# Decode attention over a long cache: K loads of 64 KB a partition into an overlapping ring, in place of two of 32 KB

## The chip, the cores and the metric

One core of a Trainium2 chip. The metric is the device time of one execution in microseconds. The kernel before takes 1271.2 us (median). A profile's span is about 2 us shorter than the run's time.

## The reference

One query token attends to a cache of 65,536 tokens, 8 key/value heads of 256 elements, two query heads to each. K and V are 268 MB each, in bfloat16. Beside it stands a small MLP over the same 448 numbers, mixed in through a gate.

```python
q = (x @ wq)                                   # 16 heads of 256
scores = einsum("bhqd,bhkd->bhqk", q, k) * Dh ** -0.5
o = einsum("bhqk,bhkd->bhqd", softmax(scores), v)
a = o @ wo
b = gelu(layernorm(x) * w1 + b1) @ w2 + b2     # the small MLP ("mixer")
out = g * a + (1 - g) * b                      # g = sigmoid(sum(x * gate_w))
```

So 537 MB must be read once, and this kernel transposes each K tile on TensorE before the scores.

## The kernel before

The cache is walked in 32 tiles `j` of 16,384 tokens: 8 MB of K and 8 MB of V, 64 KB of each a partition. K comes in two loads of 32 KB a partition, one for each half of the ring. V is one load. All go through one queue, in this order (`DC` = 4 key blocks make half a tile, `BODY` = 8):

```python
kring = sb([P, 2, DC * NT, DH], bf16, "kring")        # 2 x 32 KB a partition
vbuf = sb([P, NV, DH], bf16, "vbuf")                  # 64 KB a partition
...
for j in range(NP):                                   # the queue's engine
    for a in range(2):
        if j >= 1:
            eng.wait_ge(sem_tr[NB - 1], BODY * (j - 1) + DC * (a + 1))
        eng.dma_start(kring[:, a]..., k_src(2 * j + a)).then_inc(sem_k[a], 16)
    if j == 0:
        eng.wait_ge(s_q, 1)
    else:
        eng.wait_ge(sem_pv, j)                        # values of j-1 are done
    ...
    eng.dma_start(vbuf[:, 0:n1, :]..., v_src(j, 0, n1)).then_inc(sem_v, 16)
    ...
```

TensorE does, for each tile, the keys (8 blocks, each of 16 transposes, whose copies to SBUF feed 32 score matmuls), then the values (128 matmuls). The last V is cut up: 96 of its 128 rows a partition come in one load, the rest in three small ones, whose values are computed last ("late values").

```python
def values(j, c0, u16):
    for r in range(BODY):                             # the softmax's denominators
        ...
        pe.matmul(acc[:, DENC:SELC], ones_sq[:, :], pT[:, r, :], ...)
    ...
    with pe.If(j < NP - 1):
        some(NLATE, NV)
    some(0, NLATE).then_inc(sem_pv, 1)                # 96 or 128 value matmuls in all
```

The softmax here doesn't subtract the row's maximum and nothing guards it: scores larger than these inputs give would overflow.

## Time and profile before

| | before |
|---|---|
| median | 1271.21 us (1270.63 to 1271.29) |
| span of the profile | 1269.2 us |
| main DMA queue | 99.6% of 16 engines' span |
| packets of K, 32 KB each | mean 1217.8 ns, 8192 of them |
| packets of V, 64 KB each | mean 2422.2 ns, 3968 of them |
| last packet of the last V load ends at | 1263.97 us |

The three lowest rows are counted from the packet records of the trace (start, duration and size of each). The same count shows at least 16 packets in flight, as many as there are DMA engines, all through the loop.

From the page of the kernel before: DMA's busy tenths in 40 slices, and the main queue (packets, MB, share of 16 engines' span).

```profile
DMA  9999999999999999999999999999999999999997
q1 hardware_dynamic: 16856, 544.22, 99.6%
```

Only the last slice is under nine tenths. The list of waits of the kernel before (who waited for what: us in total, times, longest us) shows the other side of it:

```profile
PE acc L310 <- DMA vbuf<-in_A_v_cache_dram: 172.5, 32, 6.3
PE kst L272 <- DMA kring<-in_A_k_cache_dram: 120.3, 30, 5.9
```

TensorE waits twice in nearly every one of the 32 tiles, for V (about 5.4 us, 32 times) and for K (about 4 us, 30 times). It has time to spare; bytes have not.

The end of the kernel before, from TensorE's timeline (start us, us, engine, line, operation, out<-in, count, and in brackets the idle time before and what ended it):

```profile
1225.45 4.90 PE L310 MATMUL acc<-vbuf,pT 128*2 128x256 bf16 x128 [6.11 <-DMA vbuf<-in_A_v_cache_dram]
1235.28 5.17 PE L272 MATMUL kst<-ident,kring 128*128 128x128 f32 x32 [4.93 <-DMA kring<-in_A_k_cache_dram]
...
1257.40 0.62 PE L302 MATMUL acc<-pT,ones_sq 128*128 128x32 bf16 x8
1259.46 4.08 PE L310 MATMUL acc<-vbuf,pT 128*2 128x256 bf16 x96 [1.44 <-DMA vbuf<-in_A_v_cache_dram]
1263.70 0.95 PE L328 MATMUL sps<-pT,vbuf 128*128 128x2 bf16 x32
```

Read from the top: values of the last but one tile; 4.93 us of rest until the last K's first half has landed; the last keys; 1.44 us of rest until the big part of the last V has landed; its 96 value matmuls; the late values. What comes after the last of the data is on the path, so this end counts microsecond for microsecond. The 96 matmuls ran at a mean granted clock of 0.67 (the PEclk column of this table of stretches; the columns are busy us of each engine with counts, then clock, DMA share and GB/s):

```profile
1259.40:1263.60 4.20, 4.08 (x96) 2.62 (x96) 0.00 (x0) 0.00 (x0) 0.00 (x0) 0.67 0.82 330
```

### The profile page before, as it was taken

How to read it: one execution, taken by the hardware profiler on the slowest of the kernel's cores; microseconds unless marked ns; L12 is line 12 of the kernel's file. 1: busy time of each engine (PE TensorE's matmuls, PEld its weight loads, DVE VectorE, ACT ScalarE, POOL GpSimd, SP SyncE). 2: the span in 40 equal slices, each digit the busy share in tenths (PEclk: the TensorE clock that was granted, in tenths of full speed). 3: DMA queues.
4: the chain of work that ended last, by engine and by line, in shares of the span. 5: the costliest groups of instructions: out<-in, count | busy, mean ns of one | idle time of the engine just before them, and what ended most of it. 6: DMA issues, size and time to landing. Idle time of an engine off the chain costs nothing.

```text
span 1269.2 us, 37707 instructions
## 1 busy us (share of the span) xinstructions
PE 940.7 (74%) x17033; PEld 862.6 (68%) x17033; DVE 408.2 (32%) x672; ACT 535.5 (42%) x779; POOL 0.9 (0%) x7
## 2 busy tenths in 40 slices
PE   3788776878767787668776687866778666886768
PEld 3677665777657776567776677756678566876657
DVE  2454343443213332223322233322233222342223
ACT  1455433554334553335533355433455233553335
POOL 0000000000000000000000000000000000000000
PEclk9888787887878897888978789878888788897889
DMA  9999999999999999999999999999999999999997
GB/s 411 420 432 439 434 430 421 437 434 439 432 420 437 433 439 434 420 434 435 440 434 428 422 437 434 438 430 424 437 432 439 432 424 431 436 438 432 432 423 337
DMA packets 16879, 544.39 MB, mean 429 GB/s; under 512 B 1887, under 2 KB 3937, under 8 KB 4324
## 3 DMA queue, kind: packets, MB, share of 16 engines
q1 hardware_dynamic: 16856, 544.22, 99.6%
q8 instruction: 8, 0.13, 0.0%
q14 instruction: 3, 0.02, 0.0%
q10 hardware_dynamic: 12, 0.01, 0.0%
HBM read 544.22 MB, written 0.00 MB: 429 GB/s over the span
## 4 chain that ended last, share of the span: by engine, by line
DMA 85%; PE 15%; issue 0%; ACTq 0%; DVE 0%; DVEq 0%
DMA vbuf<-in_A_v_cache_dram 84%; PE acc L310 14%; DMA b_b<-in_B_b_dram 1%; PE sps L377 0%; PE sps L328 0%; PE sps L379 0%; DVE stat L457 0%; ACTq L581 0%; PE sps L335 0%; PE prj L348 0%; ACTq L585 0%; DVE out_g L576 0%; DVEq L456 0%; ACTq L584 0%; ACTq L583 0%
## 5 line engine op out<-in xcount | busy, mean ns | idle before, releaser
L605 ACT ACTIVATE ktT<-kst 128x1024 bf16<-128x1024 bf16 x512 | 499.4, 1021 | 677.6 <-PE kst L272 677.2
L272 PE MATMUL kst<-ident,kring 128*128 128x128 f32 x4096 | 554.6, 296 | 129.9 <-DMA kring<-in_A_k_cache_dram 120.3
L272 PEld LDWEIGHTS kst<-ident,kring 128*128 128x128 f32 x4096 | 505.3, 154 | 139.0 <-issue 138.5
L515 DVE COPY ktT<-kst 128x1024 bf16<-128x1024 bf16 x512 | 354.1, 692 | 737.1 <-PE kst L272 715.2
L310 PE MATMUL acc<-vbuf,pT 128*2 128x256 bf16 x4064 | 179.5, 359 | 172.5 <-DMA vbuf<-in_A_v_cache_dram 172.5
L310 PEld LDWEIGHTS acc<-vbuf,pT 128*2 128x2 bf16 x4064 | 116.4, 109 | 229.2 <-DMA vbuf<-in_A_v_cache_dram 175.6
L284 PEld LDWEIGHTS sps<-qcur,ktT 128*128 128x128 bf16 x8192 | 238.1, 96 | 3.3 <-issue 0.7
L284 PE MATMUL sps<-qcur,ktT 128*128 128x2 bf16 x8192 | 236.8, 163 | 0.6 <-issue 0.6
L596 ACT ACTIVATE pT<-sps 128x32 bf16<-128x32 f32 x256 | 51.8, 202 | 12.4 <-PE sps L284 12.4
L520 DVE COPY accs<-acc 128x288 f32<-128x288 f32 x8 | 3.7, 458 | 91.1 <-PE acc L310 91.1
L302 PE MATMUL acc<-pT,ones_sq 128*128 128x32 bf16 x256 | 16.5, 178 | 3.2
L611 ACT ACTIVATE z_b<-z_b 128x896 bf16<-128x896 bf16 x7 | 6.6, 949 | 20.9 <-DVE z_b L503 20.9
L302 PEld LDWEIGHTS acc<-pT,ones_sq 128*128 128x128 bf16 x256 | 10.9, 96 | 6.4 <-ACT pT L596 6.4
L365 PE MATMUL acc<-ones_sq,gu 1*128 1x1 bf16 x42 | 1.3, 161 | 8.6 <-DMA b_b<-in_B_b_dram 8.6
L365 PEld LDWEIGHTS acc<-ones_sq,gu 1*128 1x128 bf16 x42 | 1.2, 99 | 8.7 <-DMA b_b<-in_B_b_dram 8.7
L340 PE MATMUL acc<-zrow,ones_sq 1*128 1x292 bf16 x9 | 2.7, 305 | 4.7 <-DVE accs L520 4.0
L340 PEld LDWEIGHTS acc<-zrow,ones_sq 1*128 1x128 bf16 x9 | 0.9, 97 | 7.4 <-DVE accs L520 6.1
L348 PE MATMUL prj<-wo_sb,oTn 128*1 128x112 bf16 x128 | 2.9, 211 | 3.2 <-DVE oTn L531 3.2
L508 DVE TENSOR_TENSOR gu<-wtmp,z_b 128x896 bf16 x7 | 4.4, 625 | 1.2 <-issue 1.2
L497 DVE TENSOR_TENSOR z_b<-wtmp,u_b 128x896 bf16<-128x896 bf16 x7 | 4.4, 626 | 0.5
L501 DVE TENSOR_TENSOR z_b<-u_b,wtmp 128x896 bf16<-128x896 bf16 x7 | 4.4, 625 | 0.5
L495 DVE TENSOR_TENSOR wtmp<-u_b 128x896 bf16<-128x896 bf16 x7 | 4.4, 625 | 0.5
(82 smaller groups left out, 73.5 us busy)
## 6 DMA issues: line engine op xcount, KB each, us to landing
kring<-in_A_k_cache_dram SPq DMA_DIRECT2D x64, 4096.0 KB, 27.5
vbuf<-in_A_v_cache_dram SPq DMA_DIRECT2D x1, 6144.0 KB, 29.0
wo_sb<-in_A_wo_dram SPq DMA_DIRECT2D x8, 448.0 KB, 32.2
vbuf<-in_A_wq_dram SPq DMA_DIRECT2D x1, 3072.0 KB, 10.4
vbuf<-in_A_v_cache_dram SPq DMA_DIRECT2D x1, 1024.0 KB, 31.1
vbuf<-in_A_v_cache_dram SPq DMA_DIRECT2D x1, 768.0 KB, 32.5
vbuf<-in_A_wq_dram SPq DMA_DIRECT2D x1, 512.0 KB, 11.2
vbuf<-in_A_v_cache_dram SPq DMA_DIRECT2D x31, 33.4
```

Of the source, the lines that this page charges most:

```text
L272: ins = pe.transpose(kst[:, b, j * P:(j + 1) * P], kring_f[:, a, r * NT + 4 * b + j, :], ident[:, :])
L284: ins = pe.matmul(sps[:, par, 2 * nt:2 * nt + 2], ktT[:, par, b, ntl * DH + dj:(ntl + 1) * DH:2], qcur[:, dj, :], start=(dj == 0), stop=(d ...
L302: pe.matmul(acc[:, DENC:SELC], ones_sq[:, :], pT[:, r, :], start=False, stop=(r == BODY - 1), skip_group_check=True)
L310: ins = pe.matmul(acc[o:o + REP, 0:DH], pT[:, r, 2 * nt:2 * nt + 2], vbuf[:, n, :], start=False, stop=False, skip_group_check=True)
L495: vec.tensor_tensor(W, U, U, op=ALU.mult)
L497: vec.tensor_tensor(Z, W, U, op=ALU.mult)
L501: vec.tensor_tensor(Z, U, W, op=ALU.add)
L508: vec.tensor_tensor(gu[:, bass.ds(kt, MT), :], W, Z, op=ALU.mult).then_inc(s_pb, 1)
L515: vec.tensor_copy(ktT[:, k % KTB, b, :], kst_b[:, b, :]).then_inc(sem_ev[b], 1)
L596: act.activation(pT[:, k, :], sps[:, k % 2, 0:2 * NT], AF.Exp, scale=scale).then_inc(sem_exp, 1)
L605: act.activation(ktT[:, k % KTB, b, :], kst_b[:, b, :], AF.Copy).then_inc(sem_ev[b], 1)
L611: act.activation(z_b[:, :, :], z_b[:, :, :], AF.Tanh).then_inc(s_tanh, 1)
```

## The change

K is to come in whole tiles, with packets as large as V's. Instead of two whole buffers (128 KB) the ring has 96 KB: even tiles lie in its first 64 KB, odd ones in its last 64 KB, and the middle 32 KB belong to both. TensorE takes the shared middle first, so that the next load can be issued after 4 of 8 blocks, as before. To make room, small tensors move into V's buffer, which is free at the start, and the mixer keeps one tile at a time and sums in PSUM. Fillers (`spin`, matmuls whose result nobody reads) are put ahead of the last keys (14) and of the last values (8), meant to hold the TensorE clock up. The core of the diff (cut; the mixer, parameters and scratch space left out):

```diff
-        kring = sb([P, 2, DC * NT, DH], bf16, "kring")
+        kring = sb([P, NV + HV, DH], bf16, "kring")              # HV = NV // 2
...
             for j in range(NP):
-                for a in range(2):
-                    if j >= 1:
-                        eng.wait_ge(sem_tr[NB - 1], BODY * (j - 1) + DC * (a + 1))
-                    eng.dma_start(kring[:, a]..., k_src(2 * j + a)).then_inc(sem_k[a], 16)
+                last = j == NP - 1
+                if j >= 1:
+                    eng.wait_ge(sem_tr[NB - 1], BODY * (j - 1) + DC)
+                load(kring, A_k_cache, j, 0, HV if last else NV, HV * (j % 2), sem_k)
+                if last:
+                    load(kring, A_k_cache, j, HV, NV, HV, sem_kb)
...
+                if k < DC:
+                    tiles(HV)                    # the shared middle first
+                else:
+                    with pe.If(x2 == 0):
+                        tiles(0)
+                    with pe.Else():
+                        tiles(NV)
...
             def values(j, c0, u16):
+                pe.wait_ge(sem_exp, c0 + (BODY + 2))
                 for r in range(BODY):
-                    if r >= BODY - 2:
-                        pe.wait_ge(sem_exp, c0 + (r + 3))
...
                 with pe.If(j < NP - 1):
                     some(NLATE, NV)
+                with pe.Else():
+                    spin(8)
                 some(0, NLATE).then_inc(sem_pv, 1)
...
+                    with pe.If(j == NP - 2):
+                        spin(14)                 # ahead of the last keys
```

More of the change, by code (lines that the diff above doesn't have):

```diff
@@ L60, in bass_gated_mix__gqa_block_cached__mixer_token_mlp__decode_kernel @@
     HALF = NQ // 2
-    assert WF * NQ + HALF <= NV * DH
     NLATE = 96
@@ L75, in bass_gated_mix__gqa_block_cached__mixer_token_mlp__decode_kernel @@
     GC1 = 0.044677734375
-    MT = 2
-    NMIX = FT // MT
-    assert NMIX * MT == FT and NMIX <= NP - PPH
+    assert FT <= NP - PPH
+    HV = NV // 2
+    assert NP % 2 == 0
     DENC = DH
@@ L97, in new_sem @@
             return ctx.enter_context(nc.semaphore(name))
-        kring = sb([P, 2, DC * NT, DH], bf16, "kring")
+        kring = sb([P, NV + HV, DH], bf16, "kring")
         kring_f = kring.bitcast(f32)
         vbuf = sb([P, NV, DH], bf16, "vbuf")
+        vbuf_f = vbuf.bitcast(f32)
         ktT = sb([P, KTB, NB, 1024], bf16, "ktT")
@@ L110, in bass_gated_mix__gqa_block_cached__mixer_token_mlp__decode_kernel, with scratch @@
         early = vbuf[:, :, :].rearrange("p n d -> p (n d)")
+        early_f = vbuf_f[:, :, :].rearrange("p n d -> p (n d)")
         wq_a = early[:, 0:WF * NQ].rearrange("p (j n) -> p j n", j=WF)
         wq_b = early[:, WF * NQ:WF * NQ + HALF]
-        gu = sb([P, FT, DM], bf16, "gu")
-        early = gu[:, :, :].rearrange("p k n -> p (k n)")
-        w1row_b = early[0:1, 0:F]
-        b1row_b = early[0:1, F:2 * F]
-        w2row_b = early[0:1, 2 * F:3 * F]
+        used = [WF * NQ + HALF]
+        def scratch(rows, n, dt=bf16):
+            o = used[0]
+            used[0] += n if dt == bf16 else 2 * n
+            assert used[0] <= NV * DH and n % 2 == 0
+            return early[0:rows, o:o + n] if dt == bf16 else early_f[0:rows, o // 2:o // 2 + n]
+        wrows_b = scratch(3 * FT, P)
+        identb = scratch(3 * FT, 3 * FT)
+        xrem = scratch(1, 2 * P).rearrange("p (a n) -> p a n", a=2)
+        xrow_b = scratch(1, DM)
+        grow_b = scratch(1, DM)
+        xcb_row = scratch(1, DM)
+        h_row = scratch(1, DM)
+        prod_b = scratch(1, DM)
+        xrow = scratch(1, DM, f32)
+        xc_row = scratch(1, DM, f32)
+        scr_row = scratch(1, DM, f32)
+        gu = sb([P, DM], bf16, "gu")
+        w2cur = sb([P, 1], bf16, "w2cur")
         xcol = sb([P, WF + 2], bf16, "xcol")
-        xrem = sb([1, 2, P], bf16, "xrem")
         oTn = sb([P, 2 * REP], bf16, "oTn")
@@ L122, in bass_gated_mix__gqa_block_cached__mixer_token_mlp__decode_kernel @@
         sel = sb([P, REP], f32, "sel")
-        zrow = sb([1, 512], bf16, "zrow")
+        zrow = sb([1, NACC], bf16, "zrow")
         rden = sb([P, REP], f32, "rden")
         densum = sb([P, REP], f32, "densum")
-        xrow_b = sb([1, DM], bf16, "xrow_b")
-        grow_b = sb([1, DM], bf16, "grow_b")
         b2_b = sb([1, 1], bf16, "b2_b")
-        xrow = sb([1, DM], f32, "xrow")
-        xc_row = sb([1, DM], f32, "xc_row")
-        xcb_row = sb([1, DM], bf16, "xcb_row")
-        h_row = sb([1, DM], bf16, "h_row")
         stat = sb([1, 8], f32, "stat")
@@ L137, in bass_gated_mix__gqa_block_cached__mixer_token_mlp__decode_kernel @@
         hbT = sb([P, DM], bf16, "hbT")
-        u_b = sb([P, MT, DM], bf16, "u_b")
-        z_b = sb([P, MT, DM], bf16, "z_b")
-        wtmp = sb([P, MT, DM], bf16, "wtmp")
-        run = sb([1, DM], f32, "run")
+        u_b = sb([P, DM], bf16, "u_b")
+        z_b = sb([P, DM], bf16, "z_b")
+        wtmp = sb([P, DM], bf16, "wtmp")
         run_g = sb([P, WG], f32, "run_g")
         out_g = sb([P, WG], bf16, "out_g")
-        gate_c = sb([P, 1], f32, "gate_c")
-        prod_b = sb([1, DM], bf16, "prod_b")
-        scr_row = run
-        brow1 = xcb_row
-        brow = h_row
+        bcast = sb([P, 3], f32, "bcast")
+        brow1 = u_b[:, 0:WG]
+        brow = z_b[:, 0:WG]
+        assert 2 * WG <= NACC
         kst = psum([P, NB, 512], f32, "kst")
@@ L154, in bass_gated_mix__gqa_block_cached__mixer_token_mlp__decode_kernel @@
         prj = psum([P, 512], f32, "prj")
-        sem_k = [new_sem("sem_k%d" % i) for i in range(2)]
+        sem_k = new_sem("sem_k")
+        sem_kb = new_sem("sem_kb")
         sem_v = new_sem("sem_v")
@@ L172, in bass_gated_mix__gqa_block_cached__mixer_token_mlp__decode_kernel @@
         s_cp = new_sem("s_cp")
-        s_qc = new_sem("s_qc")
         s_late = new_sem("s_late")
-        s_brow = new_sem("s_brow")
-        s_run = new_sem("s_run")
-        sem_run = new_sem("sem_run")
         s_d2a = new_sem("s_d2a")
@@ L188, in bass_gated_mix__gqa_block_cached__mixer_token_mlp__decode_kernel @@
         s_pb = new_sem("s_pb")
-        s_bmm = new_sem("s_bmm")
         s_oTn = new_sem("s_oTn")
@@ L198, in bass_gated_mix__gqa_block_cached__mixer_token_mlp__decode_kernel, with src @@
         out_ap = out.rearrange("a b (q n) -> (a b q) n", q=NCG)
-        def k_src(i):
-            g, m = divmod(i // 2, PPH)
-            src = A_k_cache[0, g, m * BODY * CH:(m + 1) * BODY * CH, :].rearrange(
-                "(p a n) d -> p a (n d)", p=P, a=2)
-            return src[:, i % 2, :]
-        def v_src(j, n0=0, n1=NV):
+        def src(cache, j, n0=0, n1=NV):
             g, m = divmod(j, PPH)
-            src = A_v_cache[0, g, m * BODY * CH:(m + 1) * BODY * CH, :].rearrange("(p n) d -> p n d", p=P)
-            return src[:, n0:n1, :].rearrange("p n d -> p (n d)")
+            s = cache[0, g, m * BODY * CH:(m + 1) * BODY * CH, :].rearrange("(p n) d -> p n d", p=P)
+            return s[:, n0:n1, :].rearrange("p n d -> p (n d)")
         @block.sync
@@ L216, in _, with load @@
                           ).then_inc(sem_wq, 16)
+            def load(dst, cache, j, n0, n1, at, sem):
+                eng.dma_start(dst[:, at + n0:at + n1, :].rearrange("p n d -> p (n d)"), src(cache, j, n0, n1)
+                              ).then_inc(sem, 16)
             for j in range(NP):
-                for a in range(2):
-                    if j >= 1:
-                        eng.wait_ge(sem_tr[NB - 1], BODY * (j - 1) + DC * (a + 1))
-                    eng.dma_start(kring[:, a].rearrange("p n d -> p (n d)"), k_src(2 * j + a)
-                                  ).then_inc(sem_k[a], 16)
+                last = j == NP - 1
[4 more added lines that the diff above has]
+                    load(kring, A_k_cache, j, HV, NV, HV, sem_kb)
                 if j == 0:
                     eng.wait_ge(s_q, 1)
+                    eng.wait_ge(s_hb, 1)
                 else:
                     eng.wait_ge(sem_pv, j)
-                n1 = NV if j < NP - 1 else NLATE
-                eng.dma_start(vbuf[:, 0:n1, :].rearrange("p n d -> p (n d)"), v_src(j, 0, n1)).then_inc(sem_v, 16)
-                if j == NP - 1:
+                load(vbuf, A_v_cache, j, 0, NLATE if last else NV, 0, sem_v)
+                if last:
                     for (n0, n1), sem in zip(pieces, sem_vp):
-                        eng.dma_start(vbuf[:, n0:n1, :].rearrange("p n d -> p (n d)"),
-                                      v_src(j, n0, n1)).then_inc(sem, 16)
-                if j == NP - 2:
-                    eng.wait_ge(s_run, 1)
-                    for q in range(NCG):
-                        eng.dma_start(run_g[32 * q:32 * q + 1, :], run[0:1, q * WG:(q + 1) * WG]
-                                      ).then_inc(sem_run, 16)
+                        load(vbuf, A_v_cache, j, n0, n1, 0, sem)
                 if j % PPH == 0:
@@ L262, in _, with transposes, tiles @@
             one = ones_sq[0:1, 0:1]
-            def transposes(k, c, u16):
-                a, r = divmod(k, DC)
-                if r == 0:
-                    pe.wait_ge(sem_k[a], u16)
-                for b in range(NB):
-                    pe.wait_ge(sem_ev[b], c + 1)
-                    for j in range(4):
-                        ins = pe.transpose(kst[:, b, j * P:(j + 1) * P],
-                                           kring_f[:, a, r * NT + 4 * b + j, :], ident[:, :])
-                    ins.then_inc(sem_tr[b], 1)
+            def transposes(k, c, j, u16, x2):
+                if k == 0:
+                    pe.wait_ge(sem_k, u16)
+                if k == DC:
+                    with pe.If(j == NP - 1):
+                        pe.wait_ge(sem_kb, 16)
+                def tiles(at):
+                    for b in range(NB):
+                        pe.wait_ge(sem_ev[b], c + 1)
+                        for i in range(4):
+                            ins = pe.transpose(kst[:, b, i * P:(i + 1) * P],
+                                               kring_f[:, at + NT * (k % DC) + 4 * b + i, :], ident[:, :])
+                        ins.then_inc(sem_tr[b], 1)
+                if k < DC:
[5 more added lines that the diff above has]
+                        tiles(NV)
             def scores(k, c):
@@ L288, in scores, with keys, spin @@
                 ins.then_inc(sem_qk, 1)
-            def keys(c0, u16):
-                transposes(0, c0, u16)
+            def keys(c0, *where):
+                transposes(0, c0, *where)
                 for k in range(1, BODY):
-                    transposes(k, c0 + k, u16)
+                    transposes(k, c0 + k, *where)
                     scores(k - 1, c0 + k - 1)
                 scores(BODY - 1, c0 + BODY - 1)
+            def spin(n):
+                for _ in range(n):
+                    pe.matmul(kst[:, NB - 1, :], ones_sq[:, :], ktT[:, KTB - 1, 0, 0:512], start=True, stop=True)
             def values(j, c0, u16):
+                pe.wait_ge(sem_exp, c0 + (BODY + 2))
                 for r in range(BODY):
-                    if r >= BODY - 2:
-                        pe.wait_ge(sem_exp, c0 + (r + 3))
                     pe.matmul(acc[:, DENC:SELC], ones_sq[:, :], pT[:, r, :],
@@ L357, in _ @@
                 pe.matmul(acc[:, j:j + 1], xrow_b[0:1, j:WF * P:WF], one, start=True, stop=True)
-            pe.wait_ge(s_xrem, 1)
+            pe.wait_ge(s_xrem, 2)
             for a in range(2):
@@ L361, in _ @@
             pe.wait_ge(sem_misc, 16 * 5)
-            for ri, rowb in enumerate((w1row_b, b1row_b, w2row_b)):
-                for kt in range(FT):
-                    col = WF + 2 + ri * FT + kt
-                    ins = pe.matmul(acc[:, col:col + 1], rowb[0:1, kt * P:(kt + 1) * P], one,
-                                    start=True, stop=True)
-            ins.then_inc(s_col, 1)
+            pe.matmul(acc[:, WF + 2:WF + 2 + 3 * FT], wrows_b, identb, start=True, stop=True).then_inc(s_col, 1)
             pe.wait_ge(s_xcol, 1)
@@ L382, in _ @@
             pe.wait_ge(s_hrow, 1)
-            pe.matmul(prj[:, 0:DM], ones_sq[0:1, :], h_row[0:1, :], start=True, stop=True
-                      )
-            pe.matmul(prj[:, DM:DM + 1], ones_sq[0:1, :], statb[0:1, 5:6], start=True, stop=True
+            pe.matmul(prj[:, 0:DM], ones_sq[0:1, :], h_row, start=True, stop=True)
+            pe.matmul(prj[:, DM:DM + 3], ones_sq[0:1, :], statb[0:1, 5:8], start=True, stop=True
                       ).then_inc(s_h, 1)
@@ L389, in _ @@
             pe.wait_ge(s_hb, 1)
-            clear(prj[:, :])
+            clear(prj[:, 0:2 * WG])
+            x2_reg = pe.alloc_register("x2_reg")
+            pe.reg_mov(x2_reg, 0)
             on = OrderedEngineSet([pe.engine])
@@ L397, in _ @@
                     u16 = pe.snap(j * 16 + 16, min_val=16, max_val=16 * NP)
-                    keys(c0, u16)
+                    keys(c0, j, u16, pe.snap(x2_reg, min_val=0, max_val=NV))
                     values(j, c0, u16)
+                    with pe.If(j < FT):
+                        pe.wait_ge(s_pb, j + 1)
+                        for q in range(NCG):
+                            pe.matmul(prj[32 * q:32 * q + 1, WG:2 * WG], w2cur[:, :],
+                                      gu[:, q * WG:(q + 1) * WG], start=False, stop=True, skip_group_check=True)
+                    pe.reg_sub(x2_reg, NV, x2_reg)
+                    with pe.If(j == NP - 2):
+                        spin(14)
                 with pe.If(g < H - 1):
@@ L406, in _ @@
                     project()
-                with pe.If(g == H - 2):
-                    pe.wait_ge(s_pb, NMIX)
-                    for kt in range(FT):
-                        ins = pe.matmul(acc[0:1, 0:DM], w2p_b[:, kt:kt + 1], gu[:, kt, :],
-                                        start=(kt == 0), stop=(kt == FT - 1))
-                    ins.then_inc(s_bmm, 1)
-                    pe.wait_ge(s_brow, 1)
-                    clear(acc[:, 0:NACC])
             late_values(*pieces[0])
@@ L427, in _ @@
                 vec.sem_inc(sem_ev[b], 1)
-            vec.memset(xrem[:, :, :], 0.0)
+            vec.memset(xrem, 0.0)
             vec.memset(zrow[:, :], 0.0)
-            vec.memset(run_g[:, :], 0.0)
+            vec.wait_ge(sem_ident, 1)
+            vec.tensor_copy(identb, ident[0:3 * FT, 0:3 * FT]).then_inc(s_xrem, 1)
+            vec.reduce_sum(sel[:, :], ident[:, :].rearrange("p (j n) -> p n j", j=4)[:, 0:REP, :], axis=AX.X)
             vec.wait_ge(sem_x, 16)
@@ L434, in _ @@
             vec.tensor_copy(xrem[0:1, 1, 1:P:2], xrow_b[0:1, WF * P:DM]).then_inc(s_xrem, 1)
-            vec.tensor_copy(xrow[:, :], xrow_b[:, :])
+            vec.tensor_copy(xrow, xrow_b)
             vec.drain()
-            vec.reduce_sum(stat[:, 0:1], xrow[:, :], axis=AX.X)
+            vec.reduce_sum(stat[:, 0:1], xrow, axis=AX.X)
             vec.drain()
@@ L442, in _ @@
             vec.drain()
-            vec.tensor_scalar(xc_row[:, :], xrow[:, :], stat[:, 0:1], None, op0=ALU.subtract)
-            vec.tensor_scalar(xcb_row[:, :], xrow[:, :], stat[:, 0:1], None, op0=ALU.subtract)
+            vec.tensor_scalar(xc_row, xrow, stat[:, 0:1], None, op0=ALU.subtract)
+            vec.tensor_scalar(xcb_row, xrow, stat[:, 0:1], None, op0=ALU.subtract)
             vec.drain()
-            vec.tensor_tensor_reduce(out=scr_row[:, :], in0=xc_row[:, :], in1=xc_row[:, :],
+            vec.tensor_tensor_reduce(out=scr_row, in0=xc_row, in1=xc_row,
                                      scale=1.0 / DM, scalar=0.0, op0=ALU.mult, op1=ALU.add,
@@ L453, in _ @@
             vec.wait_ge(sem_misc, 16 * 5)
-            vec.tensor_copy(stat[:, 5:6], b2_b[:, :])
-            vec.tensor_tensor(prod_b[:, :], xrow_b[:, :], grow_b[:, :], op=ALU.mult)
+            vec.tensor_tensor(prod_b, xrow_b, grow_b, op=ALU.mult)
             vec.drain()
-            vec.reduce_sum(stat[:, 3:4], prod_b[:, :], axis=AX.X)
+            vec.reduce_sum(stat[:, 3:4], prod_b, axis=AX.X)
             vec.drain()
@@ L473, in _ @@
             vec.drain()
-            vec.tensor_copy(stat[:, 6:7], statb[:, 6:7])
-            vec.tensor_scalar(h_row[:, :], xcb_row[:, :], stat[:, 2:3], None, op0=ALU.mult
+            vec.tensor_copy(statb[:, 7:8], b2_b[:, :])
+            vec.tensor_scalar(h_row, xcb_row, stat[:, 2:3], None, op0=ALU.mult
                               ).then_inc(s_hrow, 1)
@@ L482, in mixer @@
             def mixer(j):
-                U = u_b[:, :, :]
-                W = wtmp[:, :, :]
-                Z = z_b[:, :, :]
-                kt = vec.snap(kt_reg, min_val=0, max_val=FT - MT)
+                U = u_b[:, :]
+                W = wtmp[:, :]
+                Z = z_b[:, :]
+                kt = vec.snap(kt_reg, min_val=0, max_val=FT - 1)
                 vec.drain()
-                for i in range(MT):
-                    vec.tensor_scalar(wtmp[:, i, :], hbT[:, :], params[:, bass.ds(kt + i, 1)], None, op0=ALU.mult)
+                vec.tensor_scalar(W, hbT[:, :], params[:, bass.ds(kt, 1)], None, op0=ALU.mult)
                 vec.drain()
-                for i in range(MT):
-                    vec.tensor_scalar(u_b[:, i, :], wtmp[:, i, :], params[:, bass.ds(kt + (FT + i), 1)], None,
-                                      op0=ALU.add)
+                vec.tensor_scalar(U, W, params[:, bass.ds(kt + FT, 1)], None, op0=ALU.add)
                 vec.drain()
@@ L504, in mixer @@
                 vec.tensor_scalar(W, U, 0.5, None, op0=ALU.mult)
+                vec.tensor_copy(w2cur[:, :], w2p_b[:, bass.ds(kt, 1)])
                 vec.wait_ge(s_tanh, j + 1)
@@ L507, in mixer @@
                 vec.drain()
-                vec.tensor_tensor(gu[:, bass.ds(kt, MT), :], W, Z, op=ALU.mult).then_inc(s_pb, 1)
-                vec.reg_add(kt_reg, kt_reg, MT)
+                vec.tensor_tensor(gu[:, :], W, Z, op=ALU.mult).then_inc(s_pb, 1)
+                vec.reg_add(kt_reg, kt_reg, 1)
             def evacuate(k, c):
@@ L539, in finish_head @@
                 by_head(acc[:, SELC:NACC])
-            vec.wait_ge(sem_ident, 1)
-            vec.reduce_sum(sel[:, :], ident[:, :].rearrange("p (j n) -> p n j", j=4)[:, 0:REP, :], axis=AX.X)
             vec.wait_ge(s_q, 1)
@@ L548, in _ @@
             vec.drain()
-            vec.tensor_copy(gate_c[:, :], prj[:, DM:DM + 1])
+            vec.tensor_copy(bcast[:, :], prj[:, DM:DM + 3])
             vec.tensor_copy(hbT[:, :], prj[:, 0:DM]).then_inc(s_hb, 1)
@@ L558, in _ @@
                         evacuate(k, c0 + k)
-                    with vec.If(j < NMIX):
+                    with vec.If(j < FT):
                         mixer(j)
                 finish_head(g)
-            vec.wait_ge(s_bmm, 1)
-            vec.tensor_copy(brow1[:, :], acc[0:1, 0:DM]).then_inc(s_brow, 1)
+            vec.wait_ge(s_proj, H - 1)
+            vec.tensor_copy(brow1, prj[:, WG:2 * WG])
             vec.drain()
-            vec.tensor_scalar(brow[:, :], brow1[:, :], stat[:, 5:6], None, op0=ALU.add)
+            vec.tensor_scalar(brow, brow1, bcast[:, 2:3], None, op0=ALU.add)
             vec.drain()
-            vec.tensor_scalar(run[:, :], brow[:, :], stat[:, 6:7], None, op0=ALU.mult).then_inc(s_run, 1)
+            vec.tensor_scalar(run_g[:, :], brow, bcast[:, 1:2], None, op0=ALU.mult)
             with nc.Fori(NC - NCPH, NC, BODY, engines=on) as c0:
@@ L573, in _ @@
             by_head(sps[:, 0, 0:2 * REP])
-            vec.wait_ge(sem_run, 16 * NCG)
             vec.wait_ge(s_proj, H)
-            vec.scalar_tensor_tensor(out_g[:, :], prj[:, 0:WG], gate_c[:, :], run_g[:, :],
+            vec.scalar_tensor_tensor(out_g[:, :], prj[:, 0:WG], bcast[:, 0:1], run_g[:, :],
                                      op0=ALU.mult, op1=ALU.add).then_inc(s_fin, 1)
@@ L580, in _ @@
         def _(act):
-            act.dma_start(xrow_b[:, :], x_row_ap).then_inc(sem_x, 16)
-            act.dma_start(grow_b[:, :], gate_w.rearrange("(a n) -> a n", a=1)).then_inc(sem_misc, 16)
-            act.dma_start(w1row_b[:, :], B_w1[0:1, :]).then_inc(sem_misc, 16)
-            act.dma_start(b1row_b[:, :], B_b1.rearrange("(a n) -> a n", a=1)).then_inc(sem_misc, 16)
-            act.dma_start(w2row_b[:, :], B_w2.rearrange("f a -> a f")).then_inc(sem_misc, 16)
+            act.dma_start(xrow_b, x_row_ap).then_inc(sem_x, 16)
+            act.dma_start(grow_b, gate_w.rearrange("(a n) -> a n", a=1)).then_inc(sem_misc, 16)
+            for i, w in enumerate((B_w1.rearrange("a f -> (a f)"), B_b1, B_w2.rearrange("f a -> (f a)"))):
+                act.dma_start(wrows_b[i * FT:(i + 1) * FT, :], w.rearrange("(k p) -> k p", p=P)
+                              ).then_inc(sem_misc, 16)
             act.dma_start(b2_b[:, :], B_b2.rearrange("(a n) -> a n", a=1)).then_inc(sem_misc, 16)
@@ L592, in _ @@
             act.activation(statb[:, 5:6], statb[:, 4:5], AF.Exp, scale=-1.0).then_inc(s_a2d, 1)
+            pt_reg = act.alloc_register("pt_reg")
+            act.reg_mov(pt_reg, DC)
             def weights(k, c):
+                p0 = act.snap(pt_reg, min_val=0, max_val=DC)
                 act.wait_ge(sem_qk, c + 3)
-                act.activation(pT[:, k, :], sps[:, k % 2, 0:2 * NT], AF.Exp, scale=scale
-                               ).then_inc(sem_exp, 1)
+                act.activation(pT[:, bass.ds(p0 + k % DC, 1), :].rearrange("p o n -> p (o n)"),
+                               sps[:, k % 2, 0:2 * NT], AF.Exp, scale=scale).then_inc(sem_exp, 1)
+                if k == DC - 1:
+                    act.reg_sub(pt_reg, DC, pt_reg)
             with nc.Fori(0, NP, 1, engines=OrderedEngineSet([act.engine])) as j:
@@ L608, in _ @@
                 weights(BODY - 1, c0 + (BODY - 1))
-                with act.If(j < NMIX):
+                with act.If(j < FT):
                     act.wait_ge(s_u, j + 1)
-                    act.activation(z_b[:, :, :], z_b[:, :, :], AF.Tanh).then_inc(s_tanh, 1)
+                    act.activation(z_b[:, :], z_b[:, :], AF.Tanh).then_inc(s_tanh, 1)
 _INS = ['A_x', 'A_k_cache', 'A_v_cache', 'A_wq', 'A_wo', 'B_x', 'B_w1', 'B_b1', 'B_w2', 'B_b2', 'gate_w']
```

## The prediction

> **What bounds the kernel now.** Data movement, with almost nothing left over. The queue table gives the main queue 99.6% of the 16 DMA engines' span; the slices show DMA at 9 tenths throughout, 429 GB/s on average. Counting packets in the trace, 16 are in flight at every moment from 1.8 to about 1264 us of the 1269.2 us span. The chain of waits is 84% V loads and 14% value matmuls (L310), but the latter only free the V buffer, some 14 us before the queue gets there. One period of 16.8 MB takes 38.78 us (V landings at 404.96 and 443.74). In it TensorE works 22.7 us on keys and 4.9 us on values, and waits, 172 us in total for V and 120 us for K (list of waits). [...]
>
> **What the change does.**
> 1. K packets become 64 KB, as V's are. A 32 KB packet takes 1217.8 ns and a 64 KB one 2422.2 ns, so two small ones cost 13.4 ns more than a large one. 31 K loads of 8 packets an engine: 31 x 8 x 13.4 ns = 3.3 us; from the periods (19.43 us for K, 19.35 us for V) 31 x 0.08 = 2.5 us. I take 2.9 us, all on the critical path.
> 2. Keys start after the whole 8 MB, about 9.7 us later in a period. Worked out from the durations: K lands at t, the next K load is issued at t+12 (V lands at t+19); keys end at t+23, values at t+28, so the next V is issued 10 us before the queue needs it at t+38.7. It never runs dry: no gain, no loss. TensorE's waits merge into one of about 10 us.
> 3. Small work (mixer by one tile, accumulated in PSUM; parameters transposed in one matmul; the finished row's small loads gone) is off the path, as are extra branches in the key loop.
> 4. The end: the last 96 value matmuls took 4.08 us because the granted clock was 0.5 until 1262.16; at full clock about 30 ns each, 2.9 us. The fillers should keep the clock up ([...]the trace alternates 0.5 and 1.0 in pieces of 3.4 us). Worth up to 1.2 us. But keys of the last but one tile now end 10 us later, so their values plus 14 fillers (about 3 us) push the last keys past the landing of their first half by 1 to 2 us, and branches add some. Net: -0.5 us, between -1.2 and +0.7.
>
> **Prediction.** 1271.2 - 2.9 - 0.5, about 1267.8 us; 8 times in 10 between 1266.0 and 1269.6. Faster by over 2%: 0.01; within 2%: 0.97; slower by over 2%: 0.02.
>
> **What would show it.** K packets of 65536 B at about 2422 ns; some 3970 fewer packets; DMA 9 tenths everywhere, period near 38.70 us; last load done near 1261 us. K waits of TensorE near 10 us x 31 = 300 us, V waits nearly gone. Values after the last big landing take about 3 us at a granted clock of 1.0.
>
> **What would make it wrong.** The queue running dry, if keys take over 19 us for their first half; a 64 KB K packet dearer than a V packet[...]; fillers delaying the last keys by more than they save, 1 to 3 us; a slow start, since the first keys wait for 8 MB and V's first load for the early arithmetic (about 17 us; the queue is full until 30 us).

That fillers keep the clock up was the estimate; at a clock of 1.00 the 96 values of the changed kernel took 2.79 us, 29 ns each.

## The result

The changed kernel takes 1270.83 us (median of 6, 1270.05 to 1271.33) against 1271.18 us (6 runs, 1270.63 to 1272.03). The ratio is 0.9996, with a 95% interval of 0.9983 to 1.0009: the same. Ratios here are the mean time of one kernel's fast runs over that of the other's of the same rounds, so not quite the ratio of the medians quoted. It lies 1.2 us above the top of the predicted range.

From the page of the changed kernel, the DMA slices and the main queue:

```profile
DMA  9999999999999999999999999999999999999997
q1 hardware_dynamic: 12264, 544.22, 99.4%
```

The same bytes in 4,592 fewer packets, and still nine tenths in every slice but the last. From its list of waits:

```profile
PE kst L277 <- DMA kring<-in_A_k_cache_dram: 313.6, 31, 14.6
```

The two rests of a tile have become one, 10.1 us on average, before the keys. The waits for V are gone from the list.

In the packet records the 64 KB packets (now 7,936, K and V) take 2422.8 ns, and the last packet of V ends at 1261.49 us instead of 1263.97. So the loop gave 2.5 us. But the span is only 1.1 us shorter (1268.1 us), and the median of the runs 0.35 us. TensorE's timeline at the end of the changed kernel shows where they stay (L327 is the value matmuls, L277 the transposes, L313 the fillers, L319 the denominators, L347 the late values):

```profile
1227.20 5.33 PE L327 MATMUL acc<-vbuf,pT 128*2 128x256 bf16 x128
1232.69 2.97 PE L313 MATMUL kst<-ktT,ones_sq 128*128 128x512 bf16 x13 [0.16 <-issue]
1235.50 3.78 PE L277 MATMUL kst<-ident,kring 128*128 128x128 f32 x32
...
1257.08 0.37 PE L319 MATMUL acc<-pT,ones_sq 128*128 128x32 bf16 x8 [0.40 <-ACT pT L612]
1257.59 1.67 PE L313 MATMUL kst<-ktT,ones_sq 128*128 128x512 bf16 x7
1259.19 2.79 PE L327 MATMUL acc<-vbuf,pT 128*2 128x256 bf16 x96
1262.72 0.95 PE L347 MATMUL sps<-pT,vbuf 128*128 128x2 bf16 x32 [0.73 <-issue]
```

None of these lines waits for a DMA any more. TensorE has become the last to be ready: by the landing record of this trace the first half of the last K was there at 1232.62 us, and in a run below with the same loads, where no filler stood before them, the last keys started at 1232.89 us. Here they start at 1235.50, because the values of the tile before, and then the fillers, are in the way. (One filler of each group is missing from the records.)

The 96 values of the last tile did become faster: 2.79 us at a granted clock of 1.00. The 128 values of the tile before took 5.33 us, at a clock of 0.68. The table of stretches of the changed kernel:

```profile
1227.20:1232.60 5.40, 5.33 (x131) 3.84 (x130) 0.00 (x0) 0.00 (x0) 0.00 (x0) 0.68 0.97 419
1259.20:1262.00 2.80, 2.79 (x97) 2.14 (x96) 0.00 (x0) 0.00 (x0) 0.00 (x0) 1.00 0.50 199
```

### The profile page after: what moved, and what is told of

It reads as the page before. It is cut to its first block, busy times and chain, and to the rows that moved or that the text cites. A ratio compares the mean times of both kernels' runs of the same rounds, so it can differ in the third digit from the quotient of the medians.

```text
span 1268.1 us, 38721 instructions
## 1 busy us (share of the span) xinstructions
PE 912.6 (72%) x17053; PEld 860.7 (68%) x17055; DVE 417.9 (33%) x741; ACT 537.2 (42%) x786; POOL 0.9 (0%) x7
## 3 DMA queue, kind: packets, MB, share of 16 engines
q1 hardware_dynamic: 12264, 544.22, 99.4%
## 4 chain that ended last, share of the span: by engine, by line
DMA 68%; PE 31%; issue 0%; SPq 0%; DVE 0%; ACT 0%; ACTq 0%
DMA kring<-in_A_k_cache_dram 68%; PE kst L277 25%; PE sps L297 5%; PE acc L327 1%; PE kst L313 0%; PE sps L347 0%; PE acc L319 0%; PE sps L354 0%; ACT pT L612 0%; SPq L217 0%; PE prj L367 0%; SPq L215 0%; DVE out_g L587 0%; DVE oTn L545 0%; ACTq L612 0%
## 5 line engine op out<-in xcount | busy, mean ns | idle before, releaser
L277 PE MATMUL kst<-ident,kring 128*128 128x128 f32 x4096 | 561.5, 298 | 314.7 <-DMA kring<-in_A_k_cache_dram 313.6
L277 PEld LDWEIGHTS kst<-ident,kring 128*128 128x128 f32 x4096 | 511.9, 155 | 324.3 <-issue 321.6
L327 PE MATMUL acc<-vbuf,pT 128*2 128x256 bf16 x4064 | 142.8, 309 | 3.1 <-issue 3.1
L327 PEld LDWEIGHTS acc<-vbuf,pT 128*2 128x2 bf16 x4064 | 104.8, 94 | 33.1 <-issue 3.9
L612 ACT ACTIVATE pT<-sps 128x32 f32 x256 | 51.8, 202 | 17.0 <-PE sps L297 17.0
L319 PE MATMUL acc<-pT,ones_sq 128*128 128x32 bf16 x256 | 11.7, 178 | 12.7 <-ACT pT L612 12.7
L319 PEld LDWEIGHTS acc<-pT,ones_sq 128*128 128x128 bf16 x256 | 8.6, 97 | 15.4 <-ACT pT L612 15.4
L629 ACT ACTIVATE z_b<-z_b 128x448 bf16<-128x448 bf16 x14 | 8.1, 577 | 20.4 <-DVE z_b L516 20.4
L510 DVE TENSOR_TENSOR z_b<-wtmp,u_b 128x448 bf16<-128x448 bf16 x14 | 5.5, 393 | 1.0
L522 DVE TENSOR_TENSOR gu<-wtmp,z_b 128x448 bf16<-128x448 bf16 x14 | 5.5, 392 | 1.0
L508 DVE TENSOR_TENSOR wtmp<-u_b 128x448 bf16<-128x448 bf16 x14 | 5.5, 392 | 1.0
L514 DVE TENSOR_TENSOR z_b<-u_b,wtmp 128x448 bf16<-128x448 bf16 x14 | 5.5, 392 | 1.0
```

The source lines that it names most:

```text
L277: ins = pe.transpose(kst[:, b, i * P:(i + 1) * P], kring_f[:, at + NT * (k % DC) + 4 * b + i, :], ident[:, :])
L319: pe.matmul(acc[:, DENC:SELC], ones_sq[:, :], pT[:, r, :], start=False, stop=(r == BODY - 1), skip_group_check=True)
L327: ins = pe.matmul(acc[o:o + REP, 0:DH], pT[:, r, 2 * nt:2 * nt + 2], vbuf[:, n, :], start=False, stop=False, skip_group_check=True)
L508: vec.tensor_tensor(W, U, U, op=ALU.mult)
L510: vec.tensor_tensor(Z, W, U, op=ALU.mult)
L514: vec.tensor_tensor(Z, U, W, op=ALU.add)
```

## The experiments

Theory A: the loop's gain is real and is given back at the end, since whole-tile K loads make TensorE late before the last keys and the 14 fillers there cost their full length. Theory B: unprofiled runs gain nothing in the loop. Rival A2: the 14 fillers pay for themselves through the clock. Eleven runs were made, of nine further kernels and of the changed one, five rounds each unless said otherwise; all were correct. They came in three calls, each on another chip; e1, e2 or e3 in a label is its call, and the changed kernel itself ran again in e1 alone.

### The changed kernel again (e1_again)

No edit.

> The changed kernel once more, as the reference for the other three of this call on the same chip. Theory A (the DMA's 2.5 us are won in the loop and given back at the end, because TensorE reaches the last keys late) and theory B (the loop gains nothing in unprofiled runs; the profiled one was a lucky run) both expect 1270.1 to 1271.3 us, 0 to 1 us under the kernel before. Last load done near 1261.5 us in the profile under A in every such profile; under B up to 1264.

Measured: 1270.61 us (1269.99 to 1270.97), before 1271.03 us; ratio 0.9996. The last V packet ends at 1261.46 us. The profile repeats: against the kernel before, the DMA is done 2.5 us earlier and the span ends 0.9 us earlier (1268.3 us).

### Without the 14 fillers (e1_no14, and again e3_no14)

```diff
-                    with pe.If(j == NP - 2):
-                        spin(14)
```

> The 14 fillers ahead of the last keys taken away. In the profile of the changed kernel the values before them ended at 1232.53 us, the first half of the last K load had landed at about 1232.4, and the fillers held TensorE until 1235.5. Theory A: the last keys start 2.7 us earlier, so the end is 2 to 2.7 us earlier (1268.3 us or so), as far as the last pieces of V (1261.5 us) allow. Rival A2 (the fillers pay for themselves by holding the clock up through the last keys and values): the keys lose the clock, and the end is no earlier, or up to 1 us later. Theory B: no change over 0.5 us.

Measured: 1268.01 us (1267.58 to 1269.36), 2.6 us under the changed kernel on the same chip; ratio to before 0.9981, interval 0.9967 to 0.9994. Its TensorE timeline near the last values:

```profile
1254.78 0.37 PE L319 MATMUL acc<-pT,ones_sq 128*128 128x32 bf16 x8 [0.40 <-ACT pT L610]
1255.29 1.67 PE L313 MATMUL kst<-ktT,ones_sq 128*128 128x512 bf16 x7
1257.06 2.79 PE L327 MATMUL acc<-vbuf,pT 128*2 128x256 bf16 x96
1260.09 1.11 PE L347 MATMUL sps<-pT,vbuf 128*128 128x2 bf16 x32 [0.23 <-issue]
```

The stretch table for those values:

```profile
1257.00:1259.90 2.90, 2.79 (x96) 2.17 (x96) 0.00 (x0) 0.00 (x0) 0.00 (x0) 1.00 0.96 391
```

And before them its last keys:

```profile
1232.89 3.83 PE L277 MATMUL kst<-ident,kring 128*128 128x128 f32 x32 [0.98 <-DMA kring<-in_A_k_cache_dram]
```

The last keys again wait for their load (0.98 us) and start 2.6 us earlier. Not all that follows gains as much. The 96 values start 2.1 us earlier (1257.06 against 1259.19): their load landed only at 1257.02, so here it sets their start again. The late values then gain another 0.5 us, since TensorE stands 0.23 us ahead of them instead of 0.73 (more of this under e1_half30). Their first 32 transposes take 3.83 us, against 3.78 us with the fillers: they came after no more than 0.98 us of rest, and ran as fast without any help. (In e1_none, below, they take the same 3.83 us after 1.34 us of rest, at a granted clock of 1.00 from 1233 to 1239 us.) Theory A holds, though some 0.5 us of the 2.6 may be the jump over the block of 14 and not its matmuls; the rival A2 falls for the 14.

The second time:

> The changed kernel without the 14 fillers once more, for its time against the kernel before, as the best version so far: about 1268 us, 3 us under the kernel before, with runs in two groups, near 1267.8 and near 1269.4 us (1.4 to 1.6 us apart[...]).

Measured: 1267.56 us (1267.34 to 1267.62), before 1270.61 us; ratio 0.9975, interval 0.9961 to 0.9988. The time was as expected; the two groups of runs were not there this time (all five within 0.3 us). They had shown in e1_no14 (three runs at 1267.6 to 1268.0, two at 1269.3 to 1269.4), and why stays open.

### Twice the fillers (e2_fill28)

```diff
-                        spin(14)
+                        spin(28)
```

> 28 fillers ahead of the last keys instead of 14. Theory A: each filler takes about 0.213 us of TensorE with nothing to hide it, so 14 more add 3.0 us: about 1273.6 us against 1270.6 us. If the loss without them was about the clock and not about TensorE's time, 14 more change little (under 1 us).

Measured: 1273.70 us (1273.08 to 1273.81). The changed kernel was not in this call; against its 1270.61 us in the other that is 3.1 us. In this profile the values before were fast, and still the keys wait for the fillers:

```profile
1228.19 3.66 PE L327 MATMUL acc<-vbuf,pT 128*2 128x256 bf16 x128
1232.01 5.99 PE L313 MATMUL kst<-ktT,ones_sq 128*128 128x512 bf16 x27 [0.16 <-issue]
1237.84 3.78 PE L277 MATMUL kst<-ident,kring 128*128 128x128 f32 x32
```

Taking 14 away gives 2.6 us and adding 14 costs 3.1 us, each close to the 3.0 us that they take. That the second fits so well is in part luck. In this profile the last keys start 2.3 us later than in the changed kernel's, and the end loses 1.5 us more, because the clock fell to 0.5 at 1260.80 us (clock records of its trace): the 8 fillers took 2.34 us instead of 1.67 and the 96 values 3.75 instead of 2.79. What both runs show is that no rest hides the fillers.

### No fillers at all (e1_none)

The 14 above and the `else` branch with `spin(8)` are both gone.

> Both groups of fillers (14 ahead of the last keys, 8 ahead of the last values) taken away. Theory A: as without the 14, and the last values may start up to 1.7 us earlier, where they then wait for V: 1268 to 1269 us, with the 96 values at about 4.1 us if the clock falls and 2.8 us if not. Rival A2: 1271 us or more.

Measured: 1269.76 us (1269.26 to 1270.46), 1.75 us over e1_no14. That is 0.8 us over the range expected, though the values took what was said for a fallen clock. The line that tells why:

```profile
1257.52 4.19 PE L327 MATMUL acc<-vbuf,pT 128*2 128x256 bf16 x96 [1.86 <-DMA vbuf<-in_A_v_cache_dram]
```

Here TensorE rests for 1.86 us before the 96 values, the clock falls (0.65 on average in that stretch), and they take 4.19 us instead of 2.79. (In this profile that load also landed 0.5 us later than in e1_no14, at 1257.48 us.) So the 8 fillers are worth their place: they fill a rest that is there anyway. The 14 had no rest to fill.

### The last K load but one in two halves (e1_half30), and that without the 14 (e2_half30_no14)

If the 14 fillers are to be of use, TensorE must have time ahead of the last keys. Loading the tile before in halves, too, lets its keys start earlier (by 8.7 us in the profiles).

```diff
                 if last:
                     ...
+                elif j == NP - 2:
+                    load(kring, A_k_cache, j, HV, NV, 0, sem_k)
+                    load(kring, A_k_cache, j, 0, HV, 0, sem_kc)
...
+                    with pe.If(j == NP - 2):
+                        pe.wait_ge(sem_kc, 16)
```

> The last K load but one also in two halves (as the last is), so that its keys start about 9.7 us earlier and TensorE stands idle before the last keys, where the 14 fillers then fit; nothing else changed. Theory A: the last keys start as soon as their half has landed, the tail is set by the last pieces of V, total about 1268.2 us (2.6 us under the changed kernel); DMA end unchanged within 0.2 us. Theory B: no change. If the end is not earlier although the keys start on time, theory A is wrong about what the tail waits for.

Measured: 1268.96 us (1267.84 to 1270.81), 1.65 us under the changed kernel, not the 2.4 that the expected 1268.2 us would be. The profiled run took 1268.18 us and the five spread over 3 us, so it is not settled that anything is missing. The fillers now end before K lands, and the keys start on time:

```profile
1228.95 2.97 PE L321 MATMUL kst<-ktT,ones_sq 128*128 128x512 bf16 x13 [0.16 <-issue]
1233.06 3.83 PE L285 MATMUL kst<-ident,kring 128*128 128x128 f32 x32 [1.14 <-DMA kring<-in_A_k_cache_dram]
...
1260.85 0.95 PE L355 MATMUL sps<-pT,vbuf 128*128 128x2 bf16 x32 [0.73 <-issue]
```

One cost that is left shows in the last line: ahead of the late values TensorE stands for 0.73 us with nothing to wait for, as it does in the changed kernel (0.65 us with 28 fillers), and 0.23 to 0.28 us in the kernels without the block of 14. The last tile jumps over that block just there. That the jump is the cause is an inference from these pairs, not tested by itself. One more jump was added among the keys, where TensorE stands for 0.68 us (0.16 us in the changed kernel).

> The last K load but one in two halves, and the 14 fillers gone: TensorE then stands idle for about 4 us before the last keys. If fillers are worth something where there is idle time, the last keys start at half clock: their first 32 transposes take about 5.2 us instead of 3.8 us, and the time is about 1.3 us over that with the halves and the fillers (1268.96 us), 1270 us. If they are worth nothing, it is the same within 0.3 us.

Measured: 1271.01 us (1270.63 to 1272.56); by medians 2.05 us over e1_half30, more than the 1.3 expected. The first 32 transposes, after 3.99 us of rest, took 6.07 us instead of 3.83, at a granted clock of 0.60 (mean of 1233 to 1239 us), so the start after the rest was dearer than I had it, and the last 96 values, too, ran slower (3.62 us instead of 2.79):

```profile
1232.93 6.07 PE L285 MATMUL kst<-ident,kring 128*128 128x128 f32 x32 [3.99 <-DMA kring<-in_A_k_cache_dram]
```

The same 14 fillers thus gain about 2 us (between calls) where there is a rest of 4 us to fill, and lose 2.6 us where there is none.

### The changed kernel with 32 KB packets (e2_k32)

```diff
-                load(kring, A_k_cache, j, 0, HV if last else NV, HV * (j % 2), sem_k)
+                load(kring, A_k_cache, j, 0, HV, HV * (j % 2), sem_k)
+                if not last:
+                    load(kring, A_k_cache, j, HV, NV, HV * (j % 2), sem_k)
```

(TensorE waits for both, with a count twice as high.)

> The changed kernel with each K load of 64 KB a partition cut into two DMAs of 32 KB a partition, issued back to back at the same place and waited for together: the same order, the same ring, the same fillers, only the packets are half as large (31 more loads). If the larger packets are what makes the DMA end 2.5 us earlier, the last load is done near 1264 us in the profile instead of 1261.5, and, as the tail of the changed kernel hangs on the landing of the last K, the time is 2.5 us (2 to 3.3) over the changed kernel's 1270.6 us, so about 1273 us. If the earlier end came from elsewhere (fewer small loads, the order of issue), both stay where they are.

Measured: 1273.33 us (1273.11 to 1273.63); ratio to before 1.0021, interval 1.0007 to 1.0035. The last V packet ends at 1263.90 us, and the 32 KB packets take 1217.8 ns again. The order, the ring and the fillers are those of the changed kernel; the packets (and 31 loads) alone bring 2.4 us of DMA time and 2.7 us of run time back (against the changed kernel of the first call; the kernel before took 1271.03 us there and 1271.10 us here). Theory B falls: the loop's gain is there in unprofiled runs too. And this is what the change would have cost without its main point: 2 us more than before.

### The kernel before with the 8 fillers (e2_before_spin8)

The `else` branch with `spin(8)` added to the kernel before.

> The kernel before with the 8 fillers ahead of its last values, and nothing else. There the last 96 value matmuls took 4.08 us, since the clock stood at 0.5 from 1258.74 to 1262.16 us. If the fillers hold the clock, they take 2.8 us, and the end is 0.8 us earlier (the last piece of V then sets it): 1270.3 us. If they only delay the values, it is 0 to 0.5 us later.

Measured: 1270.30 us (1270.08 to 1271.49), before 1271.10 us; ratio 0.9998, interval 0.9985 to 1.0012. The medians fit, the interval does not exclude no change: inconclusive. In the profiled run (its slowest) the 96 values did take 2.79 us, but started 1.3 us later: its last keys had started at a low clock (0.52, mean of 1233 to 1239 us, and 6.05 us for the first 32 transposes instead of 5.17), so the 8 fillers came 0.9 us later and held TensorE until 1260.8 us, past V's landing at 1259.41 us.

### Issuing K later (e3_late6 and e3_late8, three rounds)

How much does "the overlap first" buy? The wait ahead of each K load is raised from 4 blocks of the tile before to 6 or 8.

```diff
-                    eng.wait_ge(sem_tr[NB - 1], BODY * (j - 1) + DC)
+                    eng.wait_ge(sem_tr[NB - 1], BODY * (j - 1) + 6)      # or + BODY
```

> The changed kernel, but each K load is issued after 6 of the 8 key blocks of the tile before, instead of after 4 (when the overlapping half of the ring has been read). In the trace 4 blocks are done 11.0 us after a K landing; 6 would be at about 16.2 us, and the V load before it is done at 19.35 us. The queue still never runs dry: the same time as the changed kernel, 1270.6 us, within 0.7 us.

Measured: 1294.41 us (1291.60 to 1297.10), 24 us over the kernel before. The expectation was wrong. I had set the issue against the landing of V, which is the end of its slowest engine. In the packet records of one tile of this run 3 of the 16 engines have run out by 565.8 us and all but one by 566.4, while the load is issued at 565.49 us and its packets start from about 566.4 on; and the keys' blocks take longer after a rest (16.9 us for 6 in that tile, whose first 32 transposes took 6.30 us after 10.88 us of rest). In that tile the queue ran dry engine by engine, and the load came too late for the first of them, though not for the last. Idle engines are only half of the cost. Counted over the whole run, the 16 engines stood idle for 11 us each in the mean, and packets after such a pause took longer: 262 of the 64 KB packets took over 2.6 us, 3.05 us in the mean (13 such in the changed kernel), and 222 of them started within 4 us of a K issue. That is about another 10 us for each engine (262 packets, 0.63 us each, over 16 engines). Together they make up nearly all of the 21.7 us by which the span is longer than the changed kernel's. Why those packets are slower stays open.

> The changed kernel, but each K load is issued only when all 8 key blocks of the tile before are done, as a single 64 KB buffer would force; the ring and the packets stay. Keys end some 22.7 us after a landing and the first packet starts about 1 us after the issue, 4.4 us after the queue has run dry at 19.35 us: 31 gaps of about 4.4 us, about 136 us more, 1407 us (1390 to 1420). If the queue has other work then, or the gap is hidden, much less.

Measured: 1417.19 us (1415.63 to 1422.61), 10 us over the figure expected and within the range given. (The 1 us from issue to first packet: 0.74 and 1.75 us at the start of the kernel before, 565.49 and about 566.4 us in the tile of e3_late6.) Its page shows the DMA's slices losing their nines:

```profile
DMA  9889988989889898988988999998989988999887
```

So reading the shared half first is worth 147 us against a buffer that is freed only when it is empty: that part of the design is essential to it (the kernel before had the same through its halves).

## Why the prediction was wrong

- **What bounds the kernel: right.** 16 engines busy throughout, before and after; TensorE's waits merged as said (predicted about 300 us for K, measured 313.6; V's gone from the list).
- **Step 1, larger packets: right.** Predicted 2.9 us (2.5 to 3.3). Measured 2.5 us in the end of the last load, and 2.4 us of that is gone again with 32 KB packets (e2_k32), so the start and the small loads changed the end of the data by no more than 0.1 us. Fewer packets: I had counted K's alone (3,970); with what else went, it was 4,592 on the main queue.
- **Step 2, the queue never runs dry: right for the change,** but its margin is smaller than I worked out, as e3_late6 showed.
- **Step 3, small work off the path: no run here shows otherwise;** it was not tried by itself.
- **Step 4, the end, failed.** It said "Net: -0.5 us, between -1.2 and +0.7". Measured from the end of the data to the end of the span, the profiled run lost 1.4 us (2.5 won, 1.1 kept); by the medians of the runs about 2.1 us (2.5 won, 0.35 kept).

The end, in one table (us from the span's start; landings are those that the traces record for the loads):

| | before | changed | without the 14 |
|---|---|---|---|
| last packet of all V | 1263.97 | 1261.49 | 1261.51 |
| first half of last K landed | 1235.16 | 1232.62 | 1232.77 |
| last keys start | 1235.28 | 1235.50 | 1232.89 |
| big part of last V landed | 1259.42 | 1256.97 | 1257.02 |
| last 96 values start | 1259.46 | 1259.19 | 1257.06 |
| they take | 4.08 | 2.79 | 2.79 |
| late values start | 1263.70 | 1262.72 | 1260.09 |
| span | 1269.2 | 1268.1 | 1265.6 |

The term that was mis-sized is that the values of the last tile but one "plus 14 fillers (about 3 us) push the last keys past the landing of their first half by 1 to 2 us". The collision and its cause were foreseen, and the prediction even names it among what would make it wrong; the step gave it too small a size. It measured 2.9 us: the half landed at 1232.62 us and the keys started at 1235.50. A push of 1 to 2 us by 3 us of fillers needs TensorE to come free 1 to 2 us ahead of the landing. It came free at 1232.53 us, 0.1 us ahead, because the 128 values before ran at a low clock (5.33 us); where they ran as fast as the 96 values did at a clock of 1.00 (3.66 us, 29 ns each, e1_no14) it came free at 1231.91 us, 0.9 us ahead of its landing. So nearly the whole length of the fillers lay on the path. Nor did anything later take it up: the rest ahead of the last values (1.86 us in e1_none) is what the 8 fillers fill. The last keys had no need of the 14 either: without them the first 32 transposes took 3.83 us, with them 3.78.

The table gives the sum. From the landing of the big part of V to the late values the kernel before needs 4.3 us and the changed one 5.75, 1.5 us more: the values start 2.2 us after the landing, they take 1.3 us less, and TensorE stands 0.73 us ahead of the late values instead of 0.15 (the prediction's "branches add some"). The gain that was expected from the clock in the last values, up to 1.2 us, was right (1.3 us here); the 14 took it and more.

The expectation of e1_no14 put the landing of that half at about 1232.4 us; the trace of the changed kernel has 1232.62, and the difference changes nothing in the argument. Without the 14, the change gives most of what the prediction had for it: 1267.56 us against 1270.61 us on the same chip, 3.05 us or 0.25%, where the prediction had 3.4. That is the best version. The 14 cost 2.6 us.

What the runs show of the clock: over the last 96 values it was 0.65, and they took 4.19 us, after 1.86 us of rest (e1_none); it was 1.00, and they took 2.79 us, with the rest filled (e1_no14). The prediction's "pieces of 3.4 us" are not all of one length: the clock records at the end of the kernel before have pieces of 3.41, 6.83 and 20.48 us, which are 1, 2 and 6 times 3.41.

## What to carry to other kernels

Here DMA was busy throughout (99.6% and 99.4% of the 16 engines' span). Time was won by cheaper bytes (13.4 ns for each 64 KB that went as one packet instead of two, 2.5 us in all) and kept only where TensorE, behind the last bytes, was ready earlier by as much (0.35 us under the kernel before with the 14 fillers, 3.05 us without). A whole-tile load starts the work of the last tile but one late, which left no rest for fillers ahead of the last keys. That lateness did no harm by itself: whole, without the 14, the kernel took 1267.6 to 1268.0 us (two medians); in halves, 1268.96 us with them and 1271.01 us without. Look in the timeline for a rest that holds the fillers: the same 14 matmuls (about 3 us) gained 2 us over a rest of 4 us, and lost 2.6 us where the rest without them was 0.98 us. To find how late a load may be issued, look at the first of the 16 engines to run out, not at the landing: in the tile of e3_late6, 3 had run out by 565.8 us and the last not yet at 566.4.

## What the runs measured besides

- A packet of 32 KB took 1217.8 ns and one of 64 KB 2422.2 ns (kernel before), from which I estimate that a packet carries about 13 ns besides its bytes.
- The 16 engines drift apart on one queue: in one tile of the run with the later issue (e3_late6), 3 were dry at 565.8 us, 15 at 566.4 and the last was not yet, and issuing loads that late cost 24 us over 31 loads. Packets after such a pause were slower: 262 packets, 222 of them within 4 us of a K issue, took 3.05 us in the mean instead of 2.42.
- The loop held 433 GB/s (mean of 500 to 900 us in the changed kernel).
- In the changed kernel the clock fell to 0.5 at 1228.20 us, 20.48 us after it had risen, though TensorE had rested for no more than 0.4 us at a time between 1207.7 and 1228.2; the 128 values then took 5.33 us instead of 3.66. It fell so in 13 earlier tiles of the same trace, each time 20.48 us after it had risen and while the values ran. Why stays open.
- Jumping over a whole block of instructions: TensorE stood for 0.73 us ahead of the late values with a block of 14 fillers to be skipped, for 0.23 us without (seen in pairs of runs, not tried by itself).
